# Another order of the instructions on five engines: attention and two expert layers in one kernel

## The chip, the cores and the metric

The kernel runs on one core of a Trainium2 chip (trn2). The metric is the time of one execution on the device in microseconds (us). Five engines work beside each other, each through its own list of instructions in order: TensorE (PE, with its weight loads as PEld), VectorE (DVE), ScalarE (ACT), GpSimd (POOL) and SyncE (SP, which here only issues DMAs; ACT issues some too).

## The reference

Attention over q, k and v (4 batches, 8 heads, 576 positions, 64 wide) is the sum of two softmax attentions, a pooled one over means of four positions and a local one in which a query sees the positions less than four away. Two dense layers follow, on 2304 tokens of 512 values; all of it is wanted in fp32 accuracy.

```python
out_up = np.repeat(sm_attn(q_d, k_d, v_d), 4, axis=2)      # q_d, k_d, v_d: means of 4 positions
out_local = softmax(scale * q @ k.T where |i - j| < 4) @ v
x = (out_up + out_local) as [2304, 512]
h = x @ w_in                       # 512 -> 2048
y = (h * sigmoid(1.702 * h)) @ w_out   # 2048 -> 512
a, b = y @ w1, y @ w2              # 512 -> 1024 each
out = (a * b @ w3) @ moe2_w_out    # 1024 -> 1024 -> 512
```

## The kernel before, in words

**Arithmetic.** Each fp32 factor of a large product is split into a high and a low part (`split`, L301 to L303: a copy on ACT to the rounded type, then the difference on DVE or POOL), and `mm3` (L305 to L308) makes three matmuls of it, 128 x 128 weights against 512 columns. The weights arrive as 64-bit numbers in 512 KB pieces (`st`) and are decoded into fp32 (`dec`): `size_of` on ACT (L354) and three steps on DVE (`decode`, L361, L364, L367).

**Stages.** First w3 and moe2_w_out are multiplied into one matrix, w34: each piece of w3 is transposed on PE (`w34_transpose`, L760, with a copy on ACT, L761, and a difference on DVE, L762) and multiplied into four accumulators (`w34_mm`, `ps_w`). In the same time the attention of the first batch is made, one pair of heads after another. Then come five blocks of tokens: `h_step` (`ps_h`), Gelu on ACT (L811, `g_t`, then its two parts `gh`, L302, and `gl`, L303) and `y_step` (`ps_y`); the attention of the next batch runs beside each block. Last comes the second layer (`ab_step`, `o_tile`).

**One pair of heads.** q and k are loaded (`att_load`, L438, two pieces each; v at L444, and windows of v, `vw`, in `att_load_v`), transposed on PE against the identity (`t_piece`, L472, `ps_t`; copies on ACT, L473), multiplied into scores (`s_local`, L516, `ps_s`; `s_pool`, L535, `ps_sp`), put through the softmax (maximum on DVE, exponentials on ACT in `s_exp`, L496, which wait for the negated maximum `nb` of L494), transposed (`p_piece`, L578, `ps_pt`) and multiplied with v (`v_pool`, L593, `ps_vp`; `v_local`, L605, `ps_v`). The four products of attention use a part of the PE array: 64 rows and 64 columns at L516 and L535, 72 rows and 64 columns at L593 and L605. Exponential and Gelu need different tables on ACT, so that an `ACT_TABLE_LOAD` stands between them.

**The identity.** `make_identity` writes `ident` on POOL (two instructions, in masks.py). Every transpose on PE reads it. `setup` (L278) fills the masks `band` and `near` and the padding of `qd`, on POOL too.

**The order.** The code only records the instructions. What each engine does in which order is stated by the table `ORDER` (L20): for each engine the ranks of its recorded instructions, one after another ("12+3" is 12 to 15). `ACROSS` (L187, pairs "engine:rank<engine:rank") states some orders between engines. Waits for data are made from the reads and writes, whatever the order.

```python
for engine, text in ORDER.items():
    ranks = []
    for run in text.split():
        first, _, more = run.partition("+")
        ranks += range(int(first), int(first) + int(more or 0) + 1)
    assert sorted(ranks) == list(range(len(lists[engine]))), engine
    for i, j in zip(ranks, ranks[1:]):
        after(lists[engine][i], lists[engine][j])
```

Of the kernel before, what the change touches and what calls it, by code (L numbers as in the profile page):

```python
# [21 lines left out]
        "4+7 0+3 12+3 28 16+3 34 29 37 40 57+5 41+8 68+4 63 73 64 20+1 35 22+1 36 38+1 30 74+1 31 77+1 32+1 65+2 "  # L22
        "76 81 84 24 85 25 86+1 26 79+1 27 50+1 54+2 52+1 95+1 102+4 92 107 99+1 82 108 83 137 113 97 114+1 138 "
        "150 109+2 93+1 124 98 101 125 112 116+1 126 131 127+3 118 88 132 119 134 89+1 139 91 151 120 135+1 133 "
        "140+7 121+2 152+5 181 158 148+1 174 194+1 161 165 175 166 176 216 167 182 217 162 196 163 183 164 159+1 "
        "168+5 209 230 223+1 177+3 225 218 184+2 210 231 187+5 232 193 197+7 262 205+1 237 207+1 263 238+1 212+1 "
        "255 211 240 214+1 256+1 219 264 226+3 305 220+1 241 296 268 297 269 222 270 233 271 242 306 248 243 "
        "272+1 312 234 274 235+1 313 298 249+1 285+1 244 287 245 314 246+1 315 251+1 354 329 316 253+1 258+2 317 "
        "261 330+1 365 355 318 265 358 266+1 307 275+9 288+7 340+1 299+5 308+3 356 366 357 319+9 332+7 359 347 "
        "367 397 343 342 344 348 372 349 345+1 360 390 398 373 379 386+2 380 389 374 391 399 381 416+1 350 440 "  # L30
        "427 351 441+1 361 352 403+1 353 428 392 405 362 429+1 363+1 471 478 472+1 418 368+3 474 431+1 460 375+1 "
        "382+1 479 384+1 377+1 433 475 461 393+3 476 400 477 401+1 406+9 491 480 462 495 492 419+3 434 423+3 "
        "435+4 502+2 493 484 443 447+2 481+1 496 444+2 450+9 483 463+7 509 494 510 497 518+2 487 498 488+2 499+2 "
        "485+1 515+2 505+3 552+1 525 511 538 526 512+2 564 527 539 521+3 528+9 541+7 584 540 570 580 571+1 581+2 "
        "573 549 565 585 554+1 586+2 556 566 590+1 600+3 592+1 567+2 550 574 551 561 575 557 589 576 594+1 558 "
        "596 622 638+4 623+6 643 630 644 631 577 562 597 578+1 598+1 559+1 645 652+5 563 604+2 616 607+7 646+1 "
        "617+2 648 615 649+1 620 668 635 621 669 636 664 674 637 675+1 632 651 658+1 688 633 670 634 665 689+2 "
        "671 677 666+1 692+1 678 672 681 673 711 660+2 682 698+1 663 712 700 684 694+1 685+1 696+1 687 679 683 "
        "680 708+2 713 728+2 701+1 731 703 732 718 753 756 704 714 719 715+1 720 767+1 754+1 733 717 737+3 769 "
        "805 741 724 721 757+1 808 705+2 725+2 722 779 723 770 819 806 734+2 809+1 780 743+7 759+2 751+1 762+4 "  # L40
        "807 771 742 781 772 782 773+5 785+3 829 783 830+2 784 789+3 820 795 811 796 812 797 813 798+1 814 800 "
        "815 801 816 802 817 803 818 804 833+1 839 793+1 840+3 822+1 844 821 824+1 835+3 859 869+1 849 871 850+1 "
        "860+1 872 826+2 873+1 879 852 845+3 855+3 853 880 898 881 862 889 882 863 890 854 883 892 899+1 950 893 "
        "891 940 865+3 875+3 914 941 894 915 943 885+3 895+2 884 916+2 904+9 920+1 864 919 928+2 901 931+1 951 "
        "902 942 903 952 933 922+1 934+2 924 937 925+2 938+1 966+5 980+4 946+3 985 944 1010 945 956+7 972+3 964 "
        "976 965 977+2 1011+1 953+2 1013+2 1000+1 990 1002 991+1 1030 1020+4 1003 986+1 996+3 988+1 1031+1 993+2 "
        "1075 1040 1033 1050+1 1034 1052+2 1035 1025 1004+1 1043 1006 1016+3 1007+2 1044 1041 1055 1045 1059+1 "
        "1092+2 1076 1042 1089 1061 1090 1077 1026+1 1036+3 1028+1 1078+1 1062 1101+4 1046 1056+1 1047+2 1106 "
        "1063 1080 1064+10 1058 1127 1111+1 1081 1095+5 1082+6 1113+3 1091 1141+1 1144 1107+3 1143 1147+1 1145 "
        "1128 1149 1117+9 1133+7 1129 1163+1 1173 1150+1 1165 1174 1152+1 1183 1130+1 1175 1154 1132 1155 1166 "  # L50
        "1208 1167+1 1201 1156+1 1209 1184+1 1158 1210 1186+2 1146 1176 1192+4 1202+1 1159 1169+2 1160 1172 "
        "1161+1 1177+1 1211 1197 1212+1 1241 1198 1179+1 1199 1181+1 1238 1200 1239+1 1189+2 1235+1 1232 1204+3 "
        "1214+17 1233 1242 1237 1256 1268 1243 1247+1 1257+2 1250 1269 1234 1260+1 1244+1 1270+1 1246 1251 1272+1 "
        "1298+9 1249 1274+1 1253+1 1262+2 1252 1265+2 1255 1276+3 1314 1322+4 1315+5 1327 1321 1280 1328 1281 "
        "1329 1282+6 1330 1289 1308 1311 1290+1 1331 1309 1332 1310 1333 1292 1352 1312 1334 1313 1353 1293 1335 "
        "1346 1336 1295+1 1337 1297 1338 1343 1339 1354 1344+1 1347+1 1294 1340+2 1355 1382 1349 1372 1350 1383 "
        "1351 1356+1 1362+3 1384 1447 1373 1375 1366 1448+1 1367 1358 1368+2 1359+1 1371 1361 1376 1374 1427 1391 "
        "1453+1 1378+3 1388+2 1428 1392+1 1385+1 1429 1473 1394+2 1407+4 1397 1413+7 1398+8 1421+5 1433+3 1377 "
        "1430 1412 1455 1387 1450+2 1431 1482 1485 1432 1486 1483 1487 1476+1 1456+1 1479 1458 1480 1467 1488 "
        "1478 1489 1468 1490 1504 1469+2 1474+1 1481 1511 1491 1512 1472 1505 1437 1459+2 1438+3 1462 1442+1 1463 "  # L60
        "1444 1464 1445 1465 1446 1466 1492 1501 1493 1502 1494 1503 1495 1484 1496 1546 1514 1547 1506 1513 1497 "
        "1507+3 1498+2 1515 1521 1586+3 1517 1527+2 1518+1 1522+4 1530+15 1520 1516 1590 1566+1 1548 1568 1552+6 "
        "1560 1559 1561+4 1572+3 1549 1606 1550+1 1569 1609 1570+1 1612 1615+1 1591+5 1607+1 1630+2 1613 1617 "
        "1614 1640+2 1597 1643 1610 1576+3 1598+1 1580 1600 1581 1601+4 1582+3 1611 1618 1650+2 1619+10 1644 1653 "
        "1685 1645 1633 1686 1634 1636 1646+3 1637 1669+1 1654 1705 1655 1660+5 1635 1688 1656 1638 1657 1639 "
        "1658+1 1671 1706 1672 1689 1666+2 1673 1731 1674 1707 1690 1708+2 1675 1691+7 1676+8 1699+5 1711+3 1687 "
        "1725 1745 1734 1726+2 1732 1746 1748 1747 1751 1777 1752 1749+1 1753+1 1729 1755 1730 1756 1733 1757+2 "
        "1715 1737+5 1716+5 1743 1722 1744 1723+1 1760 1735 1761 1736 1778 1787+1 1779+1 1789+1 1770 1767 1791+1 "
        "1762 1768 1796 1769 1797+2 1781 1800 1828 1801+1 1771 1822+1 1772 1829 1782 1830 1803 1805 1831 1763 "
        "1773+3 1764+2 1832 1804 1833 1842+2 1806 1845 1783 1793 1784 1794+1 1785+1 1848 1825 1846 1849+1 1807 "  # L70
        "1824 1847 1808+13 1834+7 1884 1896 1826+1 1926+5 1851 1885 1897 1852 1854+1 1853 1860 1886 1857 1887 "
        "1856 1898+1 1888+1 1863 1900+1 1858 1902 1859 1869+2 1903 1890 1861+1 1872+1 1891+1 1874 1904 1893 "
        "1864+1 1905 1894 1875 1906 1866 1895 1907 1867 1876 1868 1877+3 1908 1881 1909+7 1882 1932 1883 1933+1 "
        "1938+2 1917+1 1941+3 1919+1 1945 1923 1921 1946 1956 1935 1957 1947 1922 1948 1965 1950 1966 1924 1949 "
        "1967+1 1925 1969 1936 1970 1958 1996 1974+1 1962+1 1971 1964 1972+1 1976 1937 1959 1953 1960+1 1977+1 "
        "2002 1979 1954+1 1989 1980+5 1992+3 1999 2003+5 2026 1951+1 1986+1 2009 1988 2014 1990+1 2010+3 2000+1 "
        "2015 1997 2062 1998 2020 2016 2041 2027+1 2063 2029+1 2042 2064+1 2043 2078+2 2066 2031+6 2017+2 2044+2 "
        "2081 2023 2067 2038 2047+2 2039 2024+1 2021 2040 2056+5 2068+3 2053 2022 2050+2 2054+1 2090 2072+3 2084 "
        "2102 2085 2082 2076 2083 2077 2091+2 2086 2094 2117+1 2087 2095 2088 2096+1 2119 2089 2098+2 2120 2101 "
        "2111 2121 2103 2122 2126+4 2105 2131 2104 2138 2154+3 2181+2 2106 2158+1 2107 2160+2 2108 2163 2109 2139 "  # L80
# [1113 lines left out]
```

## Time and profile before

| what | before |
|---|---|
| median of 3 runs | 861.75 us (858.49 to 862.26) |
| the profiled execution | 861.38 us |
| its span, first to last instruction | 859.3 us |
| PE busy | 832.8 us (97%) |
| PE weight loads busy | 710.1 us (83%) |
| DVE busy | 581.1 us (68%) |
| ACT busy | 393.5 us (46%) |
| POOL busy | 108.1 us (13%) |
| chain that ended last | PE 83%, DVE 6%, ACT 4%, DMA 3%, POOL 1%, issue 1% |

The profiled execution's 861.38 us are its span and 2.1 us around it. A matmul's duration in the trace holds its way through the array, so that one starts before the one ahead of it ends; a busy PE is not PE at its peak, and what a matmul costs is read from the distance between starts. Shares are averages over stages that have different bounds.

### The profile page before, as it was taken

The numbers are of one execution on the slowest core, as the hardware profiler recorded it, in microseconds if no ns is written. First come the engines' busy times: TensorE is split into PE (matmuls) and PEld (weight loads), VectorE is DVE, ScalarE is ACT, GpSimd is POOL, SyncE is SP. The second block draws the span as 40 slices with busy tenths as digits, with TensorE's granted clock in tenths as the row PEclk, the third lists the DMA queues.
The fourth block names the chain that finished last, engine by engine and source line by source line (L and its number), as shares of the span: only waits on it lengthen the run. The fifth ranks groups of instructions, "written<-read, shape, count | busy, mean of one in ns | idle before, by whom it ended". The sixth has DMA issues, their size and how long they took to land.

```text
span 859.3 us, 13664 instructions
## 1 busy us (share of the span) xinstructions
PE 832.8 (97%) x5132; PEld 710.1 (83%) x5132; DVE 581.1 (68%) x1069; ACT 393.5 (46%) x852; POOL 108.1 (13%) x105
## 2 busy tenths in 40 slices
PE   3899999999999999999999999999999999999998
PEld 2676778877877777878789988889998999999996
DVE  4997889999998876768787634334456554645550
ACT  3677678767574555444566453432113211221111
POOL 4223311211423233112000000000000000000000
PEclk9999999999999999999999999999999999999999
DMA  9588787677562346544478466405457255626422
GB/s 256 186 218 219 204 241 216 182 195 189 151 165 61 84 98 140 154 102 107 147 286 302 162 217 246 183 1 215 178 181 285 110 198 225 242 95 246 172 87 74
DMA packets 140598, 150.76 MB, mean 175 GB/s; under 512 B 86898, under 2 KB 121460, under 8 KB 136436
## 3 DMA queue, kind: packets, MB, share of 16 engines
q1 hardware_dynamic: 119424, 141.21, 51.6%
q10 hardware_dynamic: 21108, 8.69, 4.5%
q8 instruction: 40, 0.66, 0.3%
q14 instruction: 26, 0.21, 0.1%
HBM read 117.75 MB, written 32.11 MB: 174 GB/s over the span
## 4 chain that ended last, share of the span: by engine, by line
PE 83%; DVE 6%; ACT 4%; DMA 3%; POOL 1%; issue 1%; SPq 0%; ACTq 0%; DVEq 0%; POOLq 0%
PE ps_ab L308 7%; PE ps_ab L306 7%; PE ps_ab L307 7%; PE ps_h L306 7%; PE ps_y L308 7%; PE ps_y L306 7%; PE ps_h L307 7%; PE ps_y L307 7%; PE ps_h L308 7%; PE ps_o L307 4%; PE ps_o L308 4%; PE ps_o L306 4%; PE ps_pt L578 2%; PE ps_s L516 2%; PE ps_w L306 1%; ACT el L496 1%
## 5 line engine op out<-in xcount | busy, mean ns | idle before, releaser
L307 PE MATMUL ps_h<-x_t,w 128*128 128x512 f32 (+1 forms) x320 | 117.3, 372 | 0.0
L306 PE MATMUL ps_h<-x_t,w 128*128 128x512 f32 (+1 forms) x320 | 116.2, 374 | 0.7 <-ACT g_t L811 0.6
L308 PE MATMUL ps_y<-gh,w 128*128 128x512 f32 (+1 forms) x320 | 115.2, 373 | 0.0
L308 PE MATMUL ps_h<-x_t,w 128*128 128x512 f32 (+1 forms) x320 | 115.0, 370 | 0.0
L306 PE MATMUL ps_y<-gh,w 128*128 128x512 f32 (+1 forms) x320 | 113.7, 374 | 1.2 <-ACT gh L302 1.2
L307 PE MATMUL ps_y<-gl,w 128*128 128x512 f32 (+1 forms) x320 | 114.3, 374 | 0.2 <-DVE gl L303 0.2
L308 PE MATMUL ps_ab<-b_t,a_in 128*128 128x384 f32 x336 | 112.5, 335 | 0.0
L306 PE MATMUL ps_ab<-b_t,a_in 128*128 128x384 f32 x336 | 112.5, 335 | 0.0
L307 PE MATMUL ps_ab<-b_t,a_in 128*128 128x384 f32 x336 | 112.4, 334 | 0.0
L303 DVE TENSOR_TENSOR gl<-g_t,gh 128x512 fp32r<-128x512 f32 (+1 forms) x80 | 55.3, 693 | 54.4 <-ACT gh L302 54.1
L811 ACT ACTIVATE g_t<-ps_h 128x512 f32<-128x512 f32 (+1 forms) x80 | 43.9, 552 | 74.8 <-PE ps_h L308 74.1
L302 ACT ACTIVATE abh<-ab 128x384 fp32r<-128x384 f32 x24 | 12.6, 526 | 137.2 <-DVE ab L936 137.2
L306 PEld LDWEIGHTS ps_h<-x_t,w 128*128 128x128 f32 x320 | 59.7, 188 | 12.3 <-ACT g_t L811 2.2
L306 PEld LDWEIGHTS ps_y<-gh,w 128*128 128x128 f32 x320 | 59.7, 188 | 12.2 <-ACT gh L302 1.8
L308 PEld LDWEIGHTS ps_y<-gh,w 128*128 128x128 f32 x320 | 60.0, 188 | 10.5 <-issue 0.8
L307 PEld LDWEIGHTS ps_h<-x_t,w 128*128 128x128 f32 x320 | 60.1, 188 | 10.2 <-DVE x_t L303 0.7
L308 PEld LDWEIGHTS ps_h<-x_t,w 128*128 128x128 f32 x320 | 59.9, 188 | 10.1 <-issue 0.2
L307 PEld LDWEIGHTS ps_y<-gl,w 128*128 128x128 f32 x320 | 59.5, 188 | 10.2 <-DVE gl L303 0.8
L306 PEld LDWEIGHTS ps_ab<-b_t,a_in 128*128 128x128 f32 x336 | 63.1, 188 | 0.9
L307 PEld LDWEIGHTS ps_ab<-b_t,a_in 128*128 128x128 f32 x336 | 63.1, 188 | 0.9
L308 PEld LDWEIGHTS ps_ab<-b_t,a_in 128*128 128x128 f32 x336 | 63.1, 188 | 0.0
L367 DVE SCALAR_TENSOR_TENSOR dec<-dec,st 128x512 int32<-128x512 int32 x72 | 53.4, 746 | 9.2 <-ACT dec L354 7.8
(145 smaller groups left out, 1616.2 us busy)
## 6 DMA issues: line engine op xcount, KB each, us to landing
a_in<-a_d SPq DMA_DIRECT2D x24, 1792.0 KB
st<-in_moe_w_dram SPq DMA_DIRECT2D x32, 512.0 KB
a_d<-ap SPq DMA_DIRECT2D x8, 1792.0 KB
st<-in_moe_w_out_dram SPq DMA_DIRECT2D x24, 512.0 KB
st<-in_moe_w_in_dram SPq DMA_DIRECT2D x16, 512.0 KB
yr<-y_d SPq DMA_DIRECT2D x12, 384.0 KB
out_dram<-osb SPq DMA_DIRECT2D x17, 256.0 KB
s_v<-in_v_dram ACTq DMA_DIRECT2D x15, 288.0 KB
```

The lines of the kernel that those rows point to most:

```text
L302: nc.scalar.activation(hi, raw, AF.Copy)
L303: lo_eng.tensor_tensor(lo, raw, f32(hi), op=ALU.subtract)
L306: nc.tensor.matmul(ps, ll, rh, start=start, stop=False, skip_group_check=more)
L307: nc.tensor.matmul(ps, lh, rl, start=False, stop=False, skip_group_check=more)
L308: nc.tensor.matmul(ps, lh, rh, start=False, stop=stop, skip_group_check=more)
L367: nc.vector.scalar_tensor_tensor(t, t, 3, st[:, :, 0], op0=ALU.logical_shift_left, op1=ALU.bitwise_or)
L496: nc.scalar.activation(at["el", n][:, i] if i < NQB else at["ep", n][:, i - NQB], src(i), AF.Exp, bias=nb[:, i - i0:i - i0 + 1], scale=sca ...
L516: nc.tensor.matmul(ps[p, i - i0], qT[p, i * QB:(i + 1) * QB], kT[p, w0:w0 + KW], start=True, stop=True)
L578: nc.tensor.transpose(ps[:, i - i0], src, ident)
L811: nc.scalar.activation(g[:, :n], ps[:, :n], AF.Gelu_apprx_sigmoid)
```

## The change

The two tables `ORDER` and `ACROSS` have other numbers; all else is as it was, with every line three lower than before. The same instructions are issued on every engine, but for two more table loads on ACT (28 for 26), which the compiler puts where exponentials and Gelus stand in turn. On PE the order differs up to instruction 2755 of 4542, on DVE to 748 of 1071, on ACT to 608 of 790, on POOL to 99 of 110 and on SP to 346 of 419. One row of the table, and of `ACROSS`:

```diff
     "Pool": (
-        "8 15 19 13 28+1 11+1 9 0+2 16 10 14 20 17+1 21+1 24 23 26 3 25 27 30 6 31 34 32+1 35+1 39+1 37+1 43+1 "
...
+        "0 8 13 1 9 15+1 28 3 19 17 11 20 29 14 18 21 10 12 22 2 23+4 30+1 34 32+1 35+1 6 39+1 38 37 7 43 41 44 "
...
 ACROSS = (
...
-    "4:2<2:16 4:4<2:18 4:8<2:47 4:18<2:16 4:36<2:49 4:36<2:168 4:37<2:169 4:38<2:51 4:38<2:170 4:39<2:87 "
...
+    "4:16<2:49 4:18<2:16 4:27<2:48 4:35<2:87 4:36<2:51 4:36<2:168 4:37<2:169 4:38<2:170 4:42<2:86 4:43<2:171 "
```

POOL, from its first own work on, before (`s_v` and `vd` are the means of v):

```order
L287 MEMSET band 128x432
L293 ISA
L293 AFFINE_SELECT band<-band 64x72 x3
L483 TENSOR_TENSOR s_v<-s_v 72x4x128
L486 TENSOR_TENSOR vd<-s_v 72x256
L293 AFFINE_SELECT band<-band 64x288 x2
L293 AFFINE_SELECT band<-band 64x72
masks.py:197 MEMSET ident 128x128
masks.py:199 AFFINE_SELECT ident<-ident 128x128
L279 MEMSET qd 128x16
```

and with the change:

```order
masks.py:197 MEMSET ident 128x128
L284 MEMSET band 128x432
L290 ISA
L290 AFFINE_SELECT band<-band 64x72
masks.py:199 AFFINE_SELECT ident<-ident 128x128
L290 AFFINE_SELECT band<-band 64x72 x3
L480 TENSOR_TENSOR s_v<-s_v 72x4x128
```

The identity now stands ahead of the means of v. On SP, whose loads keep their order on the way, the first pieces of q and k changed places too. The head of SP before (`in_moe_w_dram` is w3), and then with the change:

```order
L337 DMA st<-in_moe_w_out_dram 128x1024
L444 DMA s_v<-in_v_dram 72x4x256
L342 DMA st<-in_moe_w_dram 128x4x256
L455 DMA vw<-in_v_dram 72x2x64
L438 DMA s_q<-in_q_dram 72x8x64 x2
L438 DMA s_k<-in_k_dram 72x8x64 x2
L337 DMA st<-in_moe_w_out_dram 128x1024 x2
```

```order
L334 DMA st<-in_moe_w_out_dram 128x1024
L441 DMA s_v<-in_v_dram 72x4x256
L339 DMA st<-in_moe_w_dram 128x4x256
L435 DMA s_k<-in_k_dram 72x8x64
L435 DMA s_q<-in_q_dram 72x8x64 x2
L334 DMA st<-in_moe_w_out_dram 128x1024
L435 DMA s_k<-in_k_dram 72x8x64
```

One piece of k is now ahead of q, a window of v is no longer there, and the second piece of k stands behind a 512 KB piece of weights. On ACT the scaling of the w3 piece (the second `dec`) now stands ahead of both copies of q's transposes, where it was between them. On PE, the products with v of the first pair of heads, before and then with the change:

```order
L593 MATMUL ps_vp<-PT,vd 64x144 x4
L308 MATMUL ps_w_301<-w,w3t 128x512
L308 MATMUL ps_w_297<-w,w3t 128x512
L605 MATMUL ps_v<-PT,vw 64x64 x3
L307 MATMUL ps_w_293<-w,w3t 128x512
L307 MATMUL ps_w_305<-w,w3t 128x512
L605 MATMUL ps_v<-PT,vw 64x64 x6
```

```order
L590 MATMUL ps_vp<-PT,vd 64x144 x3
L602 MATMUL ps_v<-PT,vw 64x64
L590 MATMUL ps_vp<-PT,vd 64x144
L602 MATMUL ps_v<-PT,vw 64x64 x9
L303 MATMUL ps_w_297<-w,w3t 128x512
L304 MATMUL ps_w_297<-w,w3t 128x512
L305 MATMUL ps_w_297<-w,w3t 128x512
```

Four runs of such products (4, 3, 6 and 9 of them) became two (14 and 8). Over the whole of PE the 592 products of attention stood in 47 runs between other matmuls and stand in 42 now; the five fewer are all among the first 500 instructions. On ACT, last, a block of exponentials of the second batch (`nb_2964` is its negated maximum), before and with the change:

```order
L811 ACTIVATE g_t_2943<-ps_h_2929 128x512
L302 ACTIVATE gh_2945<-g_t_2943 128x512
L496 ACT_TABLE_LOAD
L496 ACTIVATE el_2960,sm_2963<-el_2960,nb_2964 128x72 x7
L496 ACTIVATE ep_2961,sm_2963<-ps_sp_3018,nb_2964 128x144
```

```order
L808 ACTIVATE g_t_2943<-ps_h_2929 128x512
L493 ACT_TABLE_LOAD
L493 ACTIVATE ep_2961,sm_2963<-ps_sp_3018,nb_2964 128x144
L493 ACTIVATE el_2960,sm_2963<-el_2960,nb_2964 128x72
L299 ACTIVATE gh_2945<-g_t_2943 128x512
L493 ACTIVATE el_2960,sm_2963<-el_2960,nb_2964 128x72 x4
```

The high part `gh_2945`, which `ps_y` reads, moved from ahead of the block to behind its table load and two exponentials.

## Rows read from the trace of the kernel before

**Rows 1.** Stretches (us): length, busy time and instructions per engine, clock, DMA share, GB/s.

```profile
core 0: us, PE busy (x) PEld busy (x) DVE busy (x) ACT busy (x) POOL busy (x), PEclk, DMA share, GB/s
8.00:10.00 2.00, 0.00 (x0) 0.00 (x0) 1.34 (x2) 0.00 (x0) 1.93 (x3) 1.00 1.01 178
10.00:14.00 4.00, 1.60 (x10) 1.39 (x11) 0.69 (x1) 2.00 (x4) 3.13 (x12) 1.00 1.04 352
20.00:30.00 10.00, 8.65 (x54) 6.58 (x50) 9.11 (x20) 5.14 (x15) 1.45 (x1) 1.00 0.71 214
30.00:40.00 10.00, 7.58 (x36) 5.71 (x37) 8.89 (x14) 8.68 (x29) 5.10 (x5) 0.83 0.59 211
80.00:120.00 40.00, 37.81 (x338) 29.37 (x336) 29.99 (x57) 28.50 (x80) 12.24 (x11) 1.00 0.83 225
120.00:260.00 140.00, 139.71 (x974) 111.37 (x969) 134.67 (x239) 102.28 (x184) 29.42 (x24) 1.00 0.69 184
260.00:330.00 70.00, 67.49 (x527) 53.13 (x526) 57.86 (x106) 36.54 (x110) 22.38 (x18) 1.00 0.36 82
```

**Rows 2.** Timeline of the first 25 us: start, duration (us), idle time before it and releaser.

```profile
2.61 1.79 SPq L438 DMA_DIRECT2D s_q<-in_q_dram  x2
...
7.82 0.43 DVE L361 TENSOR_SCALAR st<-st 128x512 int32<-128x512 int32 x1 [1.12 <-DMA st<-in_moe_w_dram]
...
10.59 0.29 POOL masks.py:199 TENSOR_SCALAR_AFFINE_SELECT ident<-ident 128x128 f32<-128x128 f32 x1
...
10.93 1.22 PE L472 MATMUL ps_t<-ident,s_q 72*128 72x72 f32 x8 [10.93 <-POOL qd L279]
...
12.18 0.66 ACT L354 ACTIVATE dec<-st 128x512 f32<-128x512 f32 x1
...
13.63 1.11 PE L760 MATMUL ps_w<-ident,dec 128*128 128x128 f32 x4 [1.47 <-DVE dec L367]
...
16.15 0.79 PE L306 MATMUL ps_w<-w,w3t 128*128 128x512 f32 x1 [0.93 <-DVE w3t L762]
...
18.73 2.24 PE L516 MATMUL ps_s<-kT,qT 64*64 64x72 f32 x32
```

**Rows 3.** DMA issues of the first 30 us: KB of each.

```profile
st<-in_moe_w_out_dram SPq DMA_DIRECT2D x6, 512.0 KB
...
s_q<-in_q_dram SPq DMA_DIRECT2D x2, 144.0 KB
```

**Rows 4.** Timeline of PE, the first products with v.

```profile
55.33 0.73 PE L308 MATMUL ps_w<-w,w3t 128*128 128x512 f32 x2
55.99 0.45 PE L605 MATMUL ps_v<-PT,vw 72*64 72x64 f32 x6
56.37 0.73 PE L307 MATMUL ps_w<-w,w3t 128*128 128x512 f32 x2
...
57.95 0.80 PE L605 MATMUL ps_v<-PT,vw 72*64 72x64 f32 x18
58.68 0.50 PE L306 MATMUL ps_w<-w,w3t 128*128 128x512 f32 x1
```

**Rows 5.** Chain of waits near 285 us: start, time it adds (us).

```profile
283.76 0.87 PE ps_pt L578 x8
...
288.29 0.23 PE ps_h L308
```

**Rows 6.** Timeline of PE around 37 us.

```profile
36.73 1.06 PE L307 MATMUL ps_w<-w,w3t 128*128 128x512 f32 x2
37.58 1.06 PE L308 MATMUL ps_w<-w,w3t 128*128 128x512 f32 x2
```

**Rows 7.** Chain of waits at a change of tables, 253 us.

```profile
252.59 0.72 ACT ep L496 x4
253.31 0.02 issue
253.33 1.28 ACT L811
254.61 0.01 issue
254.62 0.61 ACT g_t L811
```

**Rows 8.** Waits of ACT and PE, 255 to 335 us: total, times, longest (us).

```profile
ACT L496 <- DVE nb L494: 6.4, 2, 4.1
...
PE ps_y L306 <- ACT gh L302: 1.2, 1, 1.2
```

343 rows, old and new, of tables (ACROSS, ORDER) are left out of this document.

## The prediction

> **What bounds the kernel now.** I read the stretches first. From 120 to 260 us PE is busy 139.71 of 140 us with DVE at 134.67, and after 330 us hardly anything waits; but from 20 to 40 us DVE is busy 9.11 and 8.89 of 10 us while PE has 8.65 and 7.58, and PE leaves 2.2 us of 40 open from 80 to 120 and 2.5 of 70 from 260 to 330 [rows 1]. So the kernel is a long queue of matmuls behind a start that PE doesn't fill: what the start is shortened by, the end comes earlier by, if PE's later work meets no new wait. Then I read the timeline of the start: PE's longest wait of all is its first. Its first transpose begins at 10.93 us, released by POOL, right after the identity's second instruction at 10.59 us [rows 2]. The reader should see that this row gives a wait of 10.93 us but not what would end it next; for that the loads must be followed.
>
> **The start, step by step.** POOL now writes the identity first. Ahead of its second half stand a fill of `band` and one small select only, and it no longer stands behind the means of v; it will be ready by about 2 us, long before q. So q decides. The piece of w3 that stands ahead landed by 7.82 us, when DVE's first step on it is released by that DMA [rows 2]. Behind it the queue now has one piece of k and then the two of q, 144 KB each [rows 3]. From 8 to 10 us, when such pieces were under way, 178 GB/s were moved [rows 1], which makes 0.8 us of each: the first piece of q lands at 7.8 + 2 x 0.8 = 9.4 us, the second at 10.2. PE's first transpose gains 10.9 - 9.4 = 1.5 us.
>
> The next step gains more. The transposes of w3 (L760) began at 13.63 us, released by DVE's decoding, and that waited for the scaling on ACT at 12.18 us, which stood behind the first copy of q's transposes [rows 2]. Now it stands ahead of both copies and can run when its piece has landed: 7.8 + 0.7 us on ACT, then the rest of two DVE steps, and the third of some 0.7, so about 10 us. L760 begins when q's eight transposes are through, at 10.2 + 0.6 = 10.8: a lead of 2.8 us. From L760 to the first large matmul (L306) it was 16.15 - 13.63 = 2.5 us [rows 2], so L306 comes at 13.3. Then the scores: they need both pieces of k, and the second now stands behind 512 KB of weights [rows 3]; 656 KB at the 352 GB/s of 10 to 14 us [rows 1] end at 10.2 + 1.9 = 12.1, at 178 GB/s at 13.9. With its transposes, its copies and three large matmuls ahead, the scores begin between 14.6 and 15.4, for 18.73 before [rows 2]: 3.3 to 4.1 us earlier. I take **3.7 us**. It is not lost at once, since DVE, nearly full from 20 to 40 us [rows 1], works on what these steps hand it. The lower end is the lead of the first transpose alone, 1.5 us; the upper end is 4.1.
>
> **The products in 42 runs.** A run of such products costs more than its matmuls. Six records of L605 take 56.37 - 55.99 = 0.38 us, eighteen take 58.68 - 57.95 = 0.73 [rows 4], so 0.029 each, and 0.38 - 6 x 0.029 = 0.2 us are left for going in. The two large matmuls between the runs take 55.99 - 55.33 = 0.66 us, where two in a row of such matmuls take 2 x 0.23 [rows 4, 5]: another 0.2 us for coming back. That is 0.4 us a run, and five runs fewer are 2.0 us. Transposes have no such price: eight in a run take 0.87 us, 0.11 each [rows 5], so that it doesn't matter in how many runs they stand. The five runs all lie in the first stretch, where PE is nearly full but DVE is too; where DVE is late, PE's saving only becomes idle time. I take **1.5 us**, between 0 and 2.0.
>
> **The clock.** Around 37 us two large matmuls take 37.58 - 36.73 = 0.85 us [rows 6], twice the 0.46 of later ones: the clock of that stretch is 0.83 on the mean [rows 1], so that it fell to its lower level (1.2 of 2.4 GHz) for a part, after PE had stood idle several times in the ten microseconds ahead. Some eight matmuls at 0.2 us more are 1.6 us. With another order these gaps lie elsewhere; I take 0, between a gain of 1.6 and a loss of 1.6.
>
> **The two table loads.** Each takes 1.28 us, and the steps beside it follow within 0.02 us [rows 7], 2.6 us on ACT. It stays under PE's work, since ACT is busy half of the time there (36.54 of 70 us [rows 1]). Without that cover the two cost 2.6 us.
>
> **Everything else that moved.** On all five engines the order differs up to the end of the last attention. Instructions and bytes are the same, so I cost it at nothing; what hides it is PE's queue, full from 120 us on. PE's idle time from 80 to 120 and from 260 to 330 us is 2.2 + 2.5 = 4.7 us [rows 1]; an order that avoids it gains at most that, one that doubles it loses as much. Between these ends I take 0, the nearest row being the full stretch from 120 to 260.
>
> **The sum** is 861.4 (the profiled execution's own time) - 3.7 - 1.5 = **856.2 us**; that execution lies 0.4 us under the median of 861.75, so the same forecast stands against the median.
>
> **The rivals.** *A, q is the next wait.* The identity's wait hid q's, and what follows takes up the rest: the lead stays at 1.5 us, and the saved runs give half a microsecond more: 861.4 - 2.0 = 859.4. For it: the first transposes are bound by q's landing in my own working, and the bytes went at half the rate just then (178 GB/s for 352 [rows 1]). Against it: the scaling that moved ahead on ACT frees L760, which is the longer chain. The Trainium skill (DMA: Bandwidth & Descriptors, Specifications) states that a transfer wants at least 512 bytes for line rate; q and k come in rows of 256 bytes, so by it these pieces stay slow wherever they stand in the queue, and the trace agrees (178 for 352 GB/s).
>
> *B, a Gelu caught behind an exponential block: slower.* In the block whose order is shown, the part of a Gelu that PE needs moved from ahead of the table load to behind it and two exponentials. The load there waits for DVE's maximum; such a wait was up to 4.1 us [rows 8]. With 1.28 us of load and 0.7 us for the two exponentials, PE's `ps_y` could stand for 6.1 us. It decides from the point where PE has no other products left: a Gelu behind such a block made it wait 1.2 us before [rows 8]. Once in full costs more than the whole gain; twice, of the four blocks of exponentials between 247 and 327 us, gives 856.2 + 12.2 = 868.4. Against it: in the next block another Gelu moved from within to ahead of it.
>
> *C, the later waits go too.* The lead carries DVE ahead, the 4.7 us of later idle time are halved (2.4) and the clock doesn't fall: 856.2 - 2.4 - 1.6 = 852.2.
>
> *D, the change doesn't do what it says.* The order is stated, not asked for, so PE does take the runs as counted; but if loads alone set the pace of the first 40 us, nothing is gained: 861.4. The rates of 214 and 211 GB/s there [rows 1], under the 352 of earlier, speak against it.
>
> **How the numbers follow.** Forecast 0.50, A 0.15, C 0.17, D 0.06, B 0.12. A measurement of this kernel can tell about 0.5% from no change, 4.3 us, so faster means under 857.4. C is faster as a whole (0.17), of the forecast's own range (853 to 859) about 0.42 of 0.50: 0.59. A, D and the forecast's rest are within 0.5%: 0.29. B is 0.12. The range of 8 in 10 runs from 850 (C with a little more) to 862.5 (D), and leaves B out.
>
> **What would show it.** Right: PE's first transpose at about 9.4 us, released by a DMA of q; L760 near 10.8 and the scores near 15 us; PE's products with v in two runs near 52 us; the same busy time of PE but for a microsecond or two. Wrong: a first transpose early and the stretch from 20 to 40 us as idle as before (A); waits of `ps_y` for `gh` of several microseconds between 240 and 330 us (B); a granted clock under 1.00 in more than one stretch.

## The result and the profile after

| what | before | changed |
|---|---|---|
| median, first comparison (4 runs each) | 860.66 us | 851.77 us (849.17 to 852.67) |
| ratio, 95% interval | 1 | 0.9893 (0.9859 to 0.9928) |
| a second comparison (22 and 6 runs) | 860.28 us | 849.01 us, ratio 0.9859 (0.9828 to 0.9890) |
| the profiled execution | 861.38 us | 849.17 us, span 847.3 us |

The changed kernel is 9 to 12 us faster; 856.2 was forecast, in a range of 850.0 to 862.5. The first comparison's median lies in it, the second's 1.0 us below it. The profiled execution of the changed kernel is one of its fastest and stands 12.0 us of span under that of before, so the traces show a little more than the medians do.

The page of the changed kernel, PE's and the engines' busy time:

```profile
PE 824.4 (97%) x5132; PEld 706.7 (83%) x5132; DVE 578.2 (68%) x1069; ACT 397.6 (47%) x854; POOL 112.1 (13%) x105
```

PE is busy 8.4 us less than before (832.8 us). So 8.4 of the 12.0 us of span are PE's busy time, and 3.6 its idle time.

Four of the stretches of [rows 1], in the changed kernel (us; length, then busy time and instructions of each engine, granted clock, DMA share, GB/s):

```profile
20.00:30.00 10.00, 7.68 (x43) 5.55 (x42) 9.84 (x22) 7.88 (x30) 2.13 (x2) 1.00 0.94 267
30.00:40.00 10.00, 9.97 (x91) 7.86 (x89) 9.84 (x18) 7.57 (x19) 3.35 (x3) 1.00 0.80 234
80.00:120.00 40.00, 38.58 (x339) 30.64 (x338) 34.91 (x65) 30.15 (x71) 8.11 (x8) 1.00 0.88 222
260.00:330.00 70.00, 70.00 (x509) 56.21 (x509) 58.21 (x102) 41.02 (x116) 22.35 (x17) 1.00 0.53 124
```

Four things are to be seen. From 20 to 30 us PE is no fuller than before (7.68 of 10 us for 8.65). From 30 to 40 us PE is busy 9.97 of 10 us where it was 7.58, and the clock, 0.83 on the mean before, is 1.00. DVE is fuller still, 9.84 of 10 us twice. And PE leaves 1.4 us open from 80 to 120 us, where it left 2.2, and nothing from 260 to 330 us, where it left 2.5.

The start, in the timeline (start, duration, idle time before it and its releaser), for [rows 2]:

```profile
1.62 0.29 POOL masks.py:199 TENSOR_SCALAR_AFFINE_SELECT ident<-ident 128x128 f32<-128x128 f32 x1
9.98 1.37 PE L469 MATMUL ps_t<-ident,s_q 72*128 72x72 f32 x8 [9.98 <-DMA s_q<-in_q_dram]
11.15 1.06 PE L757 MATMUL ps_w<-ident,dec 128*128 128x128 f32 x4
12.93 0.60 ACT L758 ACTIVATE w3t<-ps_w 128x512 fp32r<-128x512 f32 x1 [0.84 <-PE ps_t L469]
13.55 0.69 DVE L759 TENSOR_TENSOR w3t<-ps_w,w3t 128x512 fp32r<-128x512 f32 x1
14.30 1.22 PE L303 MATMUL ps_w<-w,w3t 128*128 128x512 f32 x2 [0.50 <-DVE w3t L759]
15.88 2.08 PE L513 MATMUL ps_s<-kT,qT 64*64 64x72 f32 x36
19.15 0.95 PE L532 MATMUL ps_sp<-kd,qd 64*64 64x144 f32 x12 [0.75 <-DVE kd L476]
```

The identity is there at 1.9 us, and the wait for POOL has become a wait for q's DMA that ends 0.95 us earlier. The next steps gain more, as forecast (L757 by 2.5 us, the scores by 2.85 us), but not the 3.3 to 4.1 us of my working. The first large matmul needs DVE's L759, which begins at 13.55 us, when the copy on ACT that it reads (L758, 12.93 us) has just ended. That copy begins 1.8 us after L757, and by the trace its wait ends with k's first transposes on PE; in before it began 1.15 us after L760. DVE itself was busy until 13.46 us, with a sum over q and a step of another piece, so it couldn't have begun much sooner either.

The durations also tell the level of TensorE's clock (1.2 or 2.4 GHz). The timeline of before, and three stretches of its windows:

```profile
21.67 1.76 PE L535 MATMUL ps_sp<-kd,qd 64*64 64x144 f32 x12 [0.70 <-DVE el L519]
25.36 0.63 PE L307 MATMUL ps_w<-w,w3t 128*128 128x512 f32 x1
27.74 0.39 PE L306 MATMUL ps_w<-w,w3t 128*128 128x512 f32 x1
```

```profile
10.00:18.00 8.00, 4.66 (x23) 3.96 (x24) 2.98 (x5) 4.61 (x8) 3.91 (x12) 1.00 1.07 350
30.00:36.00 6.00, 3.58 (x26) 2.55 (x26) 4.96 (x8) 6.00 (x23) 2.70 (x2) 1.00 0.79 276
36.40:39.70 3.30, 3.30 (x10) 2.55 (x9) 3.27 (x6) 2.28 (x6) 2.31 (x3) 0.50 0.25 95
```

And of the changed kernel:

```profile
10.00:18.00 8.00, 7.10 (x60) 5.75 (x60) 4.55 (x8) 4.28 (x7) 5.15 (x9) 1.00 1.07 334
```

The twelve pool scores took 1.76 us before and take 0.95 us in the changed kernel (at 19.15, above): the first ran at the lower level (1.2 GHz), the second at the higher (2.4 GHz). In the changed kernel PE is busy for 7.10 of the 8 us from 10 to 18 us, toward whose end the clock rises; in before it was busy for 4.66, and the large matmuls were at the lower level (0.63 us) up to 25.36 us and at the higher one (0.39 us) from 27.74 us. Before also had a fall, to 0.50 of full speed from 36.4 to 39.7 us, after a stretch with PE busy for 3.58 of 6 us. The clock of 1.00 that the windows show ahead of 26 us isn't borne out by these durations.

### The profile page after: what moved, and what is told of

Read it like the earlier page. It is cut to its first block, busy times and chain, and to the rows that moved or that the text cites. A ratio compares the mean times of both kernels' runs of the same rounds, so it can differ in the third digit from the quotient of the medians.

```text
span 847.3 us, 13673 instructions
## 1 busy us (share of the span) xinstructions
PE 824.4 (97%) x5132; PEld 706.7 (83%) x5132; DVE 578.2 (68%) x1069; ACT 397.6 (47%) x854; POOL 112.1 (13%) x105
## 4 chain that ended last, share of the span: by engine, by line
PE 86%; DVE 5%; DMA 3%; ACT 2%; issue 2%; ACTq 1%; SPq 0%; POOL 0%; DVEq 0%; POOLq 0%
PE ps_y L304 7%; PE ps_h L303 7%; PE ps_y L303 7%; PE ps_y L305 7%; PE ps_h L305 7%; PE ps_h L304 7%; PE ps_ab L305 7%; PE ps_ab L303 7%; PE ps_ab L304 7%; PE ps_o L304 4%; PE ps_o L305 4%; PE ps_o L303 4%; PE ps_pt L575 2%; PE ps_sp L532 1%; PE ps_v L602 1%
## 5 line engine op out<-in xcount | busy, mean ns | idle before, releaser
L300 DVE TENSOR_TENSOR gl<-g_t,gh 128x512 fp32r<-128x512 f32 (+1 forms) x80 | 52.8, 663 | 48.4 <-ACT gh L299 48.0
L299 ACT ACTIVATE gh<-g_t 128x512 fp32r<-128x512 f32 (+1 forms) x80 | 46.8, 588 | 30.7 <-PE ps_y L305 27.5
```

The source lines that it names most:

```text
L299: nc.scalar.activation(hi, raw, AF.Copy)
L300: lo_eng.tensor_tensor(lo, raw, f32(hi), op=ALU.subtract)
```

## The experiments

Two kinds of kernels tell where the time comes from: orders put together from both tables, and orders with one thing moved. In the first kind the instructions that the changed kernel issues up to a time stand first, in its order, and the others follow in the order of before, on every engine. Lines are those of each run's own kernel.

**The identity alone.** On POOL:

```diff
-        "8 15 19 13 28+1 11+1 9 0+2 16 10
+        "0+1 8 15 19 13 28+1 11+1 9 2 16 10
```

> The order of before, with one edit: on POOL the two instructions of the identity stand first. Theory S (the start's steps carry): PE's first transpose is released by q's DMA near 9.5 us instead of by POOL at 10.93, and the end comes as much earlier: 1.5 us, 859.2 for 860.7. Rival W (DVE and the loads set the pace of the first 40 us, so a lead at the start is lost at once): 860.7, no difference. Theory C (what the start gives is TensorE's clock: what counts is when it rises to its higher level, 26.1 us in before and 17.4 us in the changed kernel): no gain beyond 1.5 us unless the clock rises earlier than 26 us here; if it rises at 17 to 20 us, another 2 to 3 us, 856 to 857.

Measured: 859.65 us, ratio 0.9981 (0.9965 to 0.9997), 1.6 us faster. The timeline of PE:

```profile
9.71 1.19 PE L486 MATMUL ps_t<-ident,s_q 72*128 72x72 f32 x8 [9.71 <-DMA s_q<-in_q_dram]
17.75 2.24 PE L530 MATMUL ps_s<-kT,qT 64*64 64x72 f32 x32
20.68 1.00 PE L549 MATMUL ps_sp<-kd,qd 64*64 64x144 f32 x12 [0.70 <-DVE el L533]
```

q's DMA is the next wait, at 9.71 us, 1.2 us under before's 10.93 where I had given this step 1.5, and the scores are 1.0 us earlier. The row of before names the filling of `qd` as the releaser; that filling comes only at 9.93 us here, so it was the identity that PE waited for. The pool scores (1.00 us for 1.76) run at the higher level of the clock, but it falls again soon after:

```profile
26.80:30.20 3.40, 3.40 (x11) 2.48 (x11) 3.30 (x8) 1.95 (x10) 0.00 (x0) 0.50 0.32 100
```

So an early rise isn't all gain: the 856 to 857 that theory C gave to it didn't come, and S and C can't be told apart by the time. The rival that nothing is gained is out by a small margin only. Among the executions with a mean clock of 0.998 or more the medians are 860.0 us (14 of before) and 859.5 (10 of this order), so that a part of the 1.6 us may be fewer falls of the clock.

**The first 20 us, then the order of before.** SP's row, whose first 13 ranks are the changed ones:

```diff
-    "SP": 0 8 1 11 3 2 4+2 17 7 9 12 10 18 21 16 19+1 22 ...
+    "SP": 0 8 1 4 2+1 6 5 7 9 17 10 18 11+1 21 16 19+1 22 ...
```

> The changed order for what the changed kernel issues in its first 20 us (48 instructions on PE, 18 on DVE, 17 on ACT, 21 on POOL, 13 on SP), the order of before for all the rest. Theory S: the start's lead of 3.7 us is kept whole: 857.0 for 860.7. Theory C: the clock rises near 17.4 us as in the changed kernel, about 2.8 us of matmuls at the lower level are saved, and with the 1.4 us that PE is ahead at 20 us it is 856.5; the fall of the clock at 36 us stays, since PE's pauses from 30 to 36 us belong to the order of before. Rival W: DVE gives the lead back by 40 us: 860.0 or more.

Measured: 859.51 us, ratio 0.9971 (0.9951 to 0.9991): 2.5 us faster, 0.8 to 4.2. The interval holds the identity's 1.6 us as well as the 3.7 of my forecast, so the time doesn't decide between them. The traces say more. The group of the first products with v (times of its first and last start), in before, with the identity alone, and here:

```profile
L593 PE MATMUL ps_vp<-PT,vd x128: 286/286/338, 54.7 to 419.1; 72*64 72x144 f32 x128
L607 PE MATMUL ps_vp<-PT,vd x128: 286/286/338, 52.8 to 415.9; 72*64 72x144 f32 x128
L607 PE MATMUL ps_vp<-PT,vd x128: 286/286/338, 50.6 to 418.2; 72*64 72x144 f32 x128
```

The scores begin 3.1 us earlier than in before (15.67 for 18.73 us), and these products, with the order of before in between, 4.1 us. So a lead passes the stretch in which DVE is nearly full. How much of the 4.1 us is the start's own lead isn't shown, since the clock had its part: it rose sooner (pool scores in 0.95 us for 1.76) and stayed at 1.00 from 36.4 to 39.7 us. Most of it is lost later. PE waits 2.0 us for `xo` where before waited 1.2 (at 84.78 us), and the clock falls from 100.6 to 104.0 us:

```profile
81.61 0.28 PE L486 MATMUL ps_t<-ident,s_q 72*128 72x72 f32 x1 [1.99 <-DVE xo L623]
```

```profile
100.60:104.00 3.40, 3.28 (x12) 2.62 (x13) 3.40 (x7) 0.48 (x1) 1.47 (x2) 0.50 0.47 136
```

The last of these products is only 0.9 us ahead, and so is the end (a span of 858.5 us for 859.3). Other executions of this order took down to 856.0 us; the six with a mean clock of 0.998 or more have a median of 857.3, for 860.0 of before.

**The first 62 us, then the order of before.** The same with 282 instructions of PE.

```diff
-    "SP": 0 8 1 11 3 2 4+2 17 7 9 12 10 18 21 16 19+1 22 ...
+    "SP": 0 8 1 4 2+1 6 5 7 9 17 10 18 21 19 12 20 22+2 ...
```

> The changed order for what the changed kernel issues in its first 62 us (282 instructions on PE), the order of before for the rest. All five product runs that are fewer lie in this stretch, and no clock fall is left in it. Theory S (3.7 + 1.5): 855.5. Theory C (1.4 ahead at 20 us, 2.8 + 1.6 of clock, 1.5 of product runs): 853.4. By the profiles, PE is some 7 to 8 us ahead at 62 us: 853.

Measured: 854.83 us, ratio 0.9934 (0.9909 to 0.9958): 5.7 us faster, as my two terms together (5.2). From 20 to 62 us another 3.2 us have come, with an interval as wide. Not all five runs of products lie there, as I had expected: the traces show eight runs between 20 and 62 us in the order above and four in this one (48 and 44 in all), which at the price measured below would be 1.6 us. The fall of the clock around 37 us is gone as well (mean granted clock 1.000 in the profiled execution), which I had priced at 1.6.

**The first 230 us, then the order of before; and the reverse.** PE's rows at the seam (rank 1276 to 1295 of each list):

```diff
-    before:       1253+1 1262+2 1252 1265+2 1255 1276+3 1314 1322+4
-    changed:      1261+2 1274+2 1264+3 1277+1 1252 1279 1314 1322 1315+2 1323
+    first 230 us: 1261+2 1274+2 1264+1 1252 1266+1 1277+2 1314 1322+4
+    tail only:    1253+1 1262+2 1252 1265+1 1255 1276 1267 1277+2 1314 1322 1315+2 1323
```

> The changed order up to 230 us of the changed kernel (1284 instructions on PE), the order of before for the rest, which holds PE's pauses between 260 and 350 us. If the later waits of before belong to its order there, they come back: 3.7 us by the two profiles, 855.5 for the changed kernel's 851.8. If they came from the start's delay (each piece of work a few us later), they don't: 851.8. Against the run to 62 us this tells what the stretch from 62 to 230 us is worth: nothing by my prediction, 0.7 us by the two profiles.

> The order of before for its first 1284 instructions on PE (to 238.7 us) and what stands beside them, the changed order from there. If the later waits that are gone (3.7 us between 260 and 350 us by the two profiles) belong to the order there: 857.2 for 860.9. If they went because the start is earlier: 860.9. The run with the changed order up to 230 us came out 2.1 us above the changed kernel, which gives 858.8 here.

Measured: the first 853.95 us, ratio 0.9916 (0.9893 to 0.9939), 7.2 us faster; the second, in the second comparison of the changed kernel, 857.63 us for 860.28, ratio 0.9956 (0.9937 to 0.9975), 3.8 us faster by the ratio and 2.7 by the medians. The stretch from 260 to 330 us, first with the early start and the old order, then with the old start and the new order:

```profile
260.00:330.00 70.00, 68.07 (x490) 53.99 (x489) 54.49 (x103) 39.50 (x114) 21.61 (x18) 1.00 0.44 102
```

```profile
260.00:330.00 70.00, 70.00 (x544) 56.10 (x543) 59.77 (x111) 39.26 (x114) 24.45 (x19) 1.00 0.46 107
```

And what PE waits for between 245 and 325 us in the first of them:

```profile
PE ps_y L319 <- ACT gh L315: 1.2, 1, 1.2
PE ps_sp L548 <- DVE el L532: 0.6, 1, 0.6
PE ps_h L319 <- ACT g_t L824: 0.6, 1, 0.6
```

These are the three waits that before has between 255 and 335 us, to the tenth, `ps_y` for `gh` among them [rows 8]. They come back with the old order though the work stands some 8 us earlier, and with the new order behind the old start they are gone. So this gain is the order's own there, not something that an early start brings. One trace qualifies it: with the identity alone and otherwise the old order the wait of `ps_y` for `gh` is missing too, while 1.7 us of the other two kinds stay. What ACT does in the changed kernel is as I feared (`gh_2945` behind the exponentials), but PE has other products to do and waits for nothing.

**The price of a run.** In 21 runs of products between 100 and 330 us the large matmul behind a run is put into its middle; PE's ranks at the first:

```diff
-        533+4 541+7 565 584+2
+        533+1 565 535+2 541+7 584+2
```

> The changed kernel once more, beside the next three on one chip: 851.8 (0.989 of before). Theory C says in addition that its executions differ by falls of the clock: in those whose mean granted clock is 1.000, 849 to 851; each further fall (3.4 us at the lower level, 0.002 of the mean) costs about 1.6 us. If the clock doesn't matter, time and mean clock don't go together.

> The changed order, but in 21 of the runs of attention's products between 100 and 330 us the large matmul that follows a run stands in its middle, so that there are 63 runs for 42; nothing else moves. By the price that I read (0.4 us for going in and coming back): 21 x 0.4 = 8.4 us, 860.2 for 851.8; at 0.3 us it is 858.1. If the price lies beside other work, or is only how the starts are modelled in the trace: 851.8 to 853.

Measured on the same chip: 849.01 us for the changed kernel, 857.69 us with the runs split. That is 8.7 us for 21 runs, 0.41 us each. The timeline at one of them, whole in the changed kernel, and then split:

```profile
219.79 1.25 PE L602 MATMUL ps_v<-PT,vw 72*64 72x64 f32 x36
220.97 0.50 PE L304 MATMUL ps_h<-x_t,w 128*128 128x512 f32 x1
```

```profile
223.37 0.63 PE L602 MATMUL ps_v<-PT,vw 72*64 72x64 f32 x14
223.93 0.50 PE L304 MATMUL ps_h<-x_t,w 128*128 128x512 f32 x1
224.36 0.91 PE L602 MATMUL ps_v<-PT,vw 72*64 72x64 f32 x22
225.20 0.50 PE L303 MATMUL ps_h<-x_t,w 128*128 128x512 f32 x1
```

36 records take 220.97 - 219.79 = 1.18 us in one run; in two, with one large matmul between, 225.20 - 223.37 = 1.83. The large matmul alone is 0.23 of the difference [rows 5], the second switch 0.42. The runs split are of both kinds, scores and products with v, so the price is a mean over them.

**Fewer runs still.** Six pairs of neighbouring runs are made into one run each, by putting what stood between them ahead of the first:

```diff
-        275+7 288 283+1 356 340 366 307 289+6 299+5
+        356 340 366 307 275+7 288 283+1 289+6 299+5
```

> The changed kernel with six pairs of neighbouring runs of products made into one run each: the two to six instructions that stood between them (at 65, 84, 142, 200, 280 and 330 us) stand ahead of the first, so that there are 36 runs. By 0.41 us a run, which the split runs measured: 2.5 us faster than the changed kernel, 0.984 of before for 0.987. Against it: the first run of each pair comes up to 1.4 us later, and where DVE waits for its scores (at 65 and 84 us, where DVE is nearly full) the gain is given back: 0.986.

Measured: 852.30 us, ratio 0.9900 (0.9872 to 0.9927): no gain where 2.5 us were to come, since the changed kernel has 0.9859 and 0.9893. The traces agree: a span of 850.1 us at a clock of 1.00, for 846.3 and 847.3 us. Some 0.8 to 1.0 us of that is no work of the merging, since the scores, ahead of the first merged pair, begin at 16.71 us here and at 15.70 and 15.88 there. PE's busy time is 824.6 us for 824.4, so the saved switches don't show in it. The waits of PE from 60 to 340 us, total, times and longest:

```profile
PE ps_sp L532 <- DVE el L516: 1.5, 3, 0.6
PE ps_v L602 <- PE ps_vp L590: 0.8, 1, 0.8
```

The changed kernel has neither. And the timeline where two runs became one:

```profile
201.74 0.95 PE L532 MATMUL ps_sp<-kd,qd 64*64 64x144 f32 x12
202.62 0.71 PE L590 MATMUL ps_vp<-PT,vd 72*64 72x144 f32 x8
203.45 0.61 DVE L538 TENSOR_TENSOR ep<-ps_sp,mx 128x432 f32<-128x432 f32 x1
204.16 1.27 PE L602 MATMUL ps_v<-PT,vw 72*64 72x64 f32 x36 [0.83 <-PE ps_vp L590]
```

`ps_s`, `ps_sp`, `ps_vp` and `ps_v` share two buffers in PSUM with the transposes (`pst`, bufs=2). Without the large matmuls between, the third product stands before a buffer that hasn't been read yet: `ps_v` begins at 204.16 us, 0.1 us after DVE's last reading of `ps_sp` (L538) ends, though the trace names `ps_vp`. The large matmuls were PE's work during that wait. These waits are 2.3 us together, as much as six switches; why PE's busy time didn't fall by the 2.5 us isn't shown. Two of the six pairs join scores with products with v, and whether such a pair saves a switch at all wasn't tested.

**A warm PE.** Ahead of all else on PE:

```diff
         make_identity(nc, ident)
+        warm = psh.tile([128, 4, 128], F32, tag="h", name="ps_warm")
+        for i in range(32):
+            nc.tensor.transpose(warm[:, i % 4], ident, ident)
```

> The changed kernel with 32 more transposes of the identity on PE, ahead of all else, into a bank that nobody reads then; they run from about 2 to 9 us, in time in which PE has nothing to do. Theory C: the clock rises before q has landed, so that the matmuls from 10 to 17.4 us run at the higher level; some 2.4 us of them are lost at the lower one, of which the waits for DVE and loads keep about half: 850.6 for 851.8. Rival W (loads and DVE set the pace there): 851.8. If the added transposes are still under way when q lands, they cost up to 1 us.

Measured: 848.94 us, beside 849.01 us for the changed kernel: no difference. The timeline says why this settles little:

```profile
1.96 6.51 PE L990 MATMUL ps_warm<-ident 128*128 128x128 f32 x32 [1.96 <-POOL ident masks.py:199]
9.54 0.47 PE L469 MATMUL ps_t<-ident,s_q 72*128 72x72 f32 x4 [1.07 <-DMA s_q<-in_q_dram]
10.57 0.47 PE L469 MATMUL ps_t<-ident,s_q 72*128 72x72 f32 x4 [0.56 <-DMA s_q<-in_q_dram]
11.46 0.68 PE L469 MATMUL ps_t<-ident,s_k 72*128 72x72 f32 x4
```

The clock did rise (four transposes in 0.47 us at 9.54 and at 10.57), but after two pauses for q, of 1.07 and 0.56 us, it fell (four in 0.68 us at 11.46), and the scores ran at the lower level as without the added work (36 of them in 2.43 us at 15.73, for 2.47 and 2.08 us in the changed kernel's two traces). What a clock that stays up from 10 us on would bring was not reached.

**Does the lead at the start still count?** Two edits of the changed kernel, one that delays the start and one that hastens it. The identity late again, on POOL, and v's first load behind the weights, on SP (with its means later on POOL):

```diff
-    "Pool": 0 8 13 1 9 15+1 28 3 19 17 11 20 29 14 18 ...
+    "Pool": 8 13 9 15+1 28 3 19 17 11 20 0+1 29 14 18 ...
```

```diff
-    "SP": 0 8 1 4 2+1 6 5 7 9 17 10 18 21 19 12 ...
+    "SP": 0+1 4 2+1 6 5 7 9 17 10 18 8 21 19 12 ...
```

> The changed kernel, with one edit: on POOL the identity's two instructions stand behind the means of v and the selects that follow, so that they are ready at about 10.9 us as in before. The first transpose then begins at 10.9 for 9.6 to 10.0 us, 1.1 us late. Theory S: the end is 1.1 us later, 0.9872 of before for the 0.986 to 0.989 of the changed kernel. [...] Rival W (DVE, whose list is full from 12 us on in the changed kernel, sets the pace): DVE's first step on q's transposes is late by the same 1.1 us, so it is late as well.

> The changed kernel with v's first load (288 KB, needed by the products at 50 us) moved on SP behind the two weight pieces that are issued at 10.6 us, and its two means on POOL moved behind the second split of weights. All that stood behind v in the queue (w3, k, q) lands 288 KB earlier, at 229 GB/s 1.3 us: PE's first transpose at 8.5 us, DVE's step on q's transposes at 10.8 instead of 12.1 us. If the start still sets the end in the changed kernel: 1.3 us faster, 0.985 of before. If the pieces of weights behind it are what DVE waits for: no change, 0.9865.

Measured: 849.79 us, ratio 0.9872 (0.9842 to 0.9902), and 849.28 us, ratio 0.9863 (0.9832 to 0.9893): neither can be told from the changed kernel. The first transposes begin at 11.11 us in the late one and at 7.72 us in the hastened one. The scores of the one, and of the other:

```profile
16.85 2.48 PE L513 MATMUL ps_s<-kT,qT 64*64 64x72 f32 x36
```

```profile
13.83 2.48 PE L513 MATMUL ps_s<-kT,qT 64*64 64x72 f32 x36
```

The scores are 1.0 us later in the one and 2.05 us earlier in the other than in the changed kernel. The delay is kept: the first products with v begin at 50.8 us for 49.7 in the changed kernel. Of the lead of 2.05 us 0.9 are left there (first start 48.8 us):

```profile
L590 PE MATMUL ps_vp<-PT,vd x128: 285/287/338, 48.8 to 405.0; 72*64 72x144 f32 x128
```

Its span is 846.4 us, for 847.3 and 846.3 of the changed kernel's two traces: by these traces a further lead of 2 us at the scores is worth less than 1 us at the end. With four executions each, the times alone can't tell 1 us.

**What takes the further lead?** DVE, full from 18 to 58 us in the changed kernel, was the suspect. Its second decoding step is left out for six pieces:

```diff
                 low = st[:, :, 0]
+                early["n"] += 1
+                if 4 < early["n"] <= 10:
+                    continue
                 nc.vector.scalar_tensor_tensor(
```

> The changed kernel without the second decoding step (the sign's merge, 0.68 us on DVE) of six weight pieces that DVE decodes between 21 and 35 us; all else is as it was, so 6 x 0.68 = 4.1 us of DVE's list are left out. In the changed kernel DVE has no wait between 18.3 and 58 us. If DVE's list is what sets the pace there: the first products with v begin up to 4.1 us earlier than 49.7 us and the end comes as much earlier, 0.983 of before for the 0.987 of the changed kernel. If the loads are as late as DVE: DVE then waits for pieces of w3 and of the other weights, and the gain is 1 us or less, 0.986. If PE itself is full there: no more than its pauses from 20 to 60 us (5.2 us at most, of which some belong to PSUM banks).

Measured: 849.33 us, ratio 0.9854 (0.9824 to 0.9883), no more than the changed kernel has. The stretch in which DVE was relieved, and the group of the first products with v (the first started at 48.7 us):

```profile
26.00:32.00 6.00, 5.33 (x32) 3.92 (x30) 4.37 (x10) 6.00 (x20) 3.90 (x3) 1.00 1.00 330
```

```profile
L593 PE MATMUL ps_vp<-PT,vd x128: 286/286/338, 48.7 to 405.6; 72*64 72x144 f32 x128
```

DVE is busy 4.37 of 6 us now (5.68 in the changed kernel); ACT is busy 6.00 of 6 (5.79), and the DMA engines are at 1.00 (0.84). The products with v begin 1.0 us earlier, for 4.1 us less on DVE, and between 8 and 62 us DVE now waits 2.5 us for ACT's `dec` and `w3t`. So DVE is not the only bound between 20 and 60 us: with DVE relieved, ACT and the loads are met after about 1 us. Neither ACT nor the loads were relieved by themselves.

## Why the prediction was right, and where it wasn't

The sum was 5.2 us; 9 to 12 us came. By the ratios, up to each point of the new order: the identity 1.6 us, the first 20 us 2.5, the first 62 us 5.7, the first 230 us 7.2, all of it 9.2 and 12.1 in its two comparisons. Each has an interval of 1.4 to 3 us either way, so that differences between neighbours are rough; the direction and the large parts are not in doubt.

*The start, 3.7 us: its size and its reason stay open.* Each step of the working shows in the trace (q's DMA as the next wait, L757 released early by the scaling that moved ahead on ACT), but the scores came 2.85 us earlier, for 3.3 to 4.1: the term that I had too small is the way from L757 to the first large matmul, 3.15 us (11.15 to 14.30) where I had carried over the 2.5 of before. "It is not lost at once" isn't refuted: with the first 20 us of the new order alone, the first products with v begin 4.1 us before those of before, though the clock has an untold share in that. What reached the end of that order is 2.5 us (0.8 to 4.2), which excludes neither my 3.7 nor rival A's 1.5. A lead beyond the changed kernel's own was cut down early, from 2.05 us to 0.9 at 49 us; a delay of 1.0 us was not.

*The 42 runs, 1.5 us between 0 and 2.0: the price was right.* 0.41 us a run was measured where I had read 0.4; five runs would be 2.1 us. What the five bring in their own stretch wasn't measured apart from the rest.

*The clock, 0 between a gain and a loss of 1.6: missed.* The profiled execution shows the fall at 36 us gone (some eight matmuls, 1.6 us, as priced) and the first rise before 19.15 us instead of after 25.36 us; the twelve pool scores alone are 0.8 us cheaper for that. I had left the first rise out, since I read the clock from the windows and not from the durations. Over all executions the falls are fewer too: the mean granted clock is 0.9968 in 68 executions of before and 0.9985 in 10 of the changed kernel. Among the 68, time goes with it: 859.9 us in the median of the 36 at 0.998 or more, 862.0 in the 17 around 0.996, 864.0 in the 12 around 0.994, thus 1.6 to 2 us for 0.002. By that, an estimate, the falls make about 1.4 us of the gain. What the earlier rise gives at the end wasn't shown by itself; with the identity alone it came early as well, and was followed by a fall.

*The same busy time of PE "but for a microsecond or two": missed.* It fell by 8.4 us. The fall of the clock (1.6), the pool scores (0.8) and five runs (2.1, by their price) make 4.5 of them. The earlier rise of the clock may have more of it than those scores; the other 3.9 us aren't traced to a cause.

*Two table loads at nothing: in keeping with the trace.* From 245 to 325 us PE waits for nothing.

*All else at 0, between +4.7 and -4.7: the largest miss.* I took the full stretch from 120 to 260 us as the nearest row; the gain lies behind it, and some of it ahead. From 260 to 330 us PE is full now, and the tail's order alone is worth 2.7 to 3.8 us. From 62 to 230 us another 1.5 came by the ratios; before's wait of 1.2 us for `xo` at 84.78 us is no longer in the changed kernel's trace. Rival C had this gain (half of the 4.7 us, and the clock's 1.6) and, with 852.2, the time; but it had it from the early start, and the two orders with one half of each show that most of it is the order's own. Rival B is out: `ps_y` waits for no `gh`, though the Gelu moved as shown.

So the direction, the price of a run and the next wait were right, and the time fell near the range's lower end because two terms that I put at nothing, clock and tail, both came out as gains.

## What to carry to other kernels

Whether a lead at the start is kept is read by following one and the same group of instructions through both traces: here 4.1 us were still there behind a stretch in which DVE was nearly full, and went to a wait and to the clock later on, while a further 2 us were halved within 35 us. Where two engines and the loads are full together, relieving one gained only about 1 us. Waits late in the program can belong to the order there: an order joined from two halves tells that in one run each way. A switch between small and large matmuls has a price that two rows give, but the work between two runs may be what fills a wait for a PSUM buffer, so fewer runs are not always faster. And PE's busy time wants a forecast beside its waits: 8.4 of the 12.0 us stood there, at the same instructions.

## What the runs showed of the hardware

Entering and leaving a run of matmuls on 64 or 72 rows and 64 columns cost 0.41 us together (21 runs, 8.7 us), while a single transpose between large matmuls cost no such thing. The timeline of before:

```profile
41.35 0.39 PE L306 MATMUL ps_w<-w,w3t 128*128 128x512 f32 x1
41.58 0.23 PE L472 MATMUL ps_t<-ident,s_k 72*128 72x72 f32 x1
41.61 0.48 PE L308 MATMUL ps_w<-w,w3t 128*128 128x512 f32 x1
41.92 0.39 PE L307 MATMUL ps_w<-w,w3t 128*128 128x512 f32 x1
```

From 41.35 to 41.92 us there are two large matmuls at 0.23 and 0.11 us for the transpose, which is what one of eight in a run takes [rows 5].

The granted clock differs between executions of one program: of 68 of the kernel before, 6 stood at 0.9985 or above and 3 under 0.9935, and these 3 took 862.6, 866.2 and 866.9 us where those 6 took 859.3 to 861.1. A large matmul's duration tells the level where the clock's own rows don't: 0.63 us at the lower and 0.39 us at the higher, in a row of such matmuls. Transposes of the identity alone raised the clock by 9.54 us, and it was lost again by 11.46 us.
